# A window attention and two dense layers on one core: the first layer's low product moves to GpSimd, more words are joined there, and sums of weights are kept in DRAM

## The chip, the cores and the metric

One core of one Trainium2 chip runs the whole program. Its engines are TensorE (matrix products, PE in the profile, with PEld for the loading of weights), VectorE (DVE), ScalarE (ACT), GpSimd (POOL) and the queue that issues transfers (SP). The metric is the device time of one execution in microseconds, the median of the runs.

## What is computed

The inputs are q, k and v (float32; 4 batches, 8 heads, 576 positions, 64 columns) and two layers' weights (float64). Cut to what matters:

```python
scores = scale * q @ k.T                       # per batch and head
scores = where(0 <= i - j < 128, scores - slope[head] * (i - j), -1e9)
x = softmax(scores) @ v                        # as 2304 tokens x 512

h = x @ w_in                                   # first layer, 512 -> 2048
P = a0 + a1*h + a2*h**2 + a3*h**3
Q = 1 + |b0|*|h| + |b1|*h**2
y = (P / (Q + 1e-6)) @ w_out                   # 2048 -> 512

h = y @ w2_in                                  # second layer, 512 -> 2048
out = where(h > 0, h, exp(min(h, 0)) - 1) @ w2_out
```

## The kernel before

The weights arrive as pairs of 32-bit words of a float64. A float32 is joined from the two: ScalarE scales the high word (`conv_scale`, `join_scale`), VectorE shifts the low word, sets its bits in and sets the sign (three operations, `conv_shift`, `conv_or`, `conv_sign`, or all of `join_words`). Each float32 operand of a product is then split into a high part that TensorE can take and a low part, the difference from it; a product is three matmuls, high x high, low x high and high x low (`PASS`).

**Attention** (0 to about 155 us) works through 16 units of two heads by an order written out by hand (`STEPS`), with the words of the first layer's weights joined beside it. The words of the last four pairs of keys come by `conv_step`, six of whose calls stand at the end of attention and the rest in the first block of the first layer; the low part (`conv_lo`) was GpSimd's there.

**The first layer** (about 155 to 560 us) takes the 2304 tokens in 6 blocks of 384 columns (`j`) and the 2048 hidden columns in 16 chunks of 128 (`f`), 96 steps `s` in all. In step s TensorE runs `gemm1` for chunk s (12 matmuls into one of four banks, h) and `gemm2_T` for chunk s - 3 (12 matmuls that need the chunk's high and low product). `rational(s)` is the work between them: ScalarE forms the square, the Abs, two linear terms, and the logarithm and exponential that give 1/Q; VectorE forms the denominator of chunk s, and for chunk s - 1 the high product `hi` (L286), a correction (L298, L304) and the low product `lo` (L308), and between them, for chunk s, the numerator (L302, which reads h from PSUM, and L306). At the end of a block `split_x` splits the next block's x (four high parts on ScalarE, four low parts on VectorE, L224), since there is room for one block's. In blocks 1 to 5, the steps with f not divisible by 3 and below 15 join half a word of the second layer's weights, 40 halves in all; these go to DRAM as float32 (`joined`). In the last block `prepare` forms the second layer's first sums and splits.

**The second layer** (from about 555 us) takes the tokens in three rounds J of two blocks, and the hidden columns in 8 pairs p of two chunks, 24 pairs q in all. A pair's seven products come from sums and differences of weights (`sum_w`, four per pair, on GpSimd) and of x (`sum_x`, four pairs of rows per round, on GpSimd but in the first), each split into high and low (`hi_w`, `hi_op`, `lo`). Results are added up on VectorE (L943), go through the exponential on ScalarE and VectorE (L958), are split, and are multiplied by the second weights in the next pair (`gemm2`). Twelve of the 16 second words (`raw_ones`) were joined in the first round (`join_wo`) and kept in DRAM. The steps stand in a table (`step`) with engine, cost and needs; `in_order` lays out one order for all engines from these costs. Each engine's queue is worked off in that order.

Of the kernel before, what the change touches and what calls it, by code (L numbers as in the profile page):

```python
# [11 lines left out]
I32 = mybir.dt.int32  # L12
# [32 lines left out]
def kernel(  # L45
# [90 lines left out]
    def conv_shift(key):  # L136
        low, _ = words(key)
        nc.vector.tensor_scalar(
            out=low, in0=low, scalar1=29, scalar2=None, op0=ALU.logical_shift_right
        )  # L140

# [28 lines left out]

    stage = {"scaled": None, "whole": None}

    def conv_step(keys, more=True):
# [89 lines left out]
    def rational(c, old=True, beside=None):  # L263
# [17 lines left out]
        if old:  # L281
            qq0, ee0, rr0 = q_t.pop(c - 1)
            hi = row(f"ghi{(c - 1) % 4}", F32R)
            lo = row(f"glo{(c - 1) % 4}", F32R)
            g_t[c - 1] = (hi, lo)
            nc.vector.tensor_tensor(out=hi, in0=ee0, in1=rr0, op=ALU.mult)  # L286
        if new:
            nc.vector.scalar_tensor_tensor(  # L288
                out=qq, in0=h2, scalar=b_abs[:, 1:2], in1=qq, op0=ALU.mult, op1=ALU.add
            )  # L290
            rr = row(f"rr{c % 2}")
# [3 lines left out]
        if beside:  # L295
            beside()
# [382 lines left out]
    def experts():  # L679
# [46 lines left out]
        joined, half, two, whole, pair = {}, {}, {}, [], []  # L726
        OPS, XO, sums, G, sq, low_part = {}, {}, {}, {}, {}, {}
# [3 lines left out]
        early_ones = [("wi", KF + f) for f in range(KF)] + [("wo", KF + 2 * p) for p in range(4)]  # L731

        def load_half(n):
# [4 lines left out]
            half[n] = t = cv_tile([P, PC], I32, "half", 2 * (n % 2))  # L738
# [12 lines left out]
        def join_scale(n):  # L751
# [3 lines left out]
            if not whole:  # L755
                whole.append(cv_tile([P, 2, HC], F32, "whole", 1))
            w = whole[0][:, n % 2]
            nc.scalar.activation(out=w, in_=high.bitcast(F32), func=AF.Copy, scale=2.0 ** -112)

        def join_words(n):  # L760
            t = half.pop(n).rearrange("p (c t) -> p c t", t=2)
            low, high = t[:, :, 0], t[:, :, 1]
            w = whole[0][:, n % 2]
            nc.vector.tensor_scalar(
                out=low, in0=low, scalar1=29, scalar2=None, op0=ALU.logical_shift_right
            )
            wi = w.bitcast(I32)
            nc.vector.scalar_tensor_tensor(
                out=wi, in0=wi, scalar=3, in1=low, op0=ALU.logical_shift_left, op1=ALU.bitwise_or
            )  # L770
            nc.vector.scalar_tensor_tensor(
# [50 lines left out]
        def sum_w(q, eng=nc.gpsimd):  # L822
            w = two[q]
            a11, a12, a21, a22 = [w[:, e, h * HC:(h + 1) * HC] for e in range(2) for h in range(2)]
            sq[q] = s = [cv_tile([P, 2, HC], F32, "s", n) for n in range(2)]
            for n, (x, y, op) in enumerate((
                (a21, a22, ALU.add), (s[0][:, 0], a11, ALU.subtract), (a11, a21, ALU.subtract),
                (a12, s[0][:, 1], ALU.subtract),
            )):
                eng.tensor_tensor(out=s[n // 2][:, n % 2], in0=x, in1=y, op=op)  # L830

# [21 lines left out]
        def sum_x(J, n, eng=nc.gpsimd):  # L853

            if J == 0:
# [5 lines left out]
            for k in range(2):  # L861
# [142 lines left out]
        def weight_steps(w):  # L1004
# [5 lines left out]
            if w > 0:  # L1010
# [3 lines left out]
                step((w, "sum"), "POOL", 2900, lambda: sum_w(w), (w, "load"), (w - 1, "lo", "C"), (w - 1, "lo", "D"))  # L1014
# [26 lines left out]
        def x_sums(J):  # L1041

            used = [("xlo", J - 1, nm, k) for nm in ORDER for k in range(2)]
            for n in range(4):
                step(("sum", J, n), "POOL", 2300, lambda n=n: sum_x(J, n), *used, *[("sum", J, i) for i in range(n)])

        def second(q):
# [25 lines left out]
            if q == 0:  # L1073
                x_steps(0, ("t1", "t4", "b22"), -1)
# [5 lines left out]
            if p == NP2 - 1 and q + 1 < NQ:  # L1080
                x_sums(q // NP2 + 1)
                x_steps(q // NP2 + 1, ORDER, q)

        def in_order():
# [20 lines left out]
            free = {"PE": 0, "ACT": 1500, "DVE": 2500, "POOL": 0, "SP": 0}  # L1105
# [35 lines left out]
        def prepare(f):  # L1141

            if f == 1:
                load_wi(0)
            if 3 <= f < 7:
                sum_x(0, f - 3, nc.vector)
            if f == 7:
                sum_w(0, nc.vector)
            if 8 <= f < 12:
                hi_w(0, "ABCD"[f - 8])  # L1150
                lo((0, "ABCD"[f - 8]))
            if 7 <= f < 11:
                for k in range(2):
                    hi_op(0, ORDER[f - 7], k)
                for k in range(2):
                    lo((0, ORDER[f - 7], k))
# [72 lines left out]
```

## Time and profile before

| | us |
|---|---|
| median of 3 runs | 968.08 (966.07 to 968.5) |
| the profiled execution | 965.85 |
| its span, first to last instruction | 963.8 |
| TensorE busy | 927.3 (96%) |
| VectorE busy | 864.8 (90%) |
| ScalarE busy | 750.6 (78%) |
| GpSimd busy | 232.7 (24%) |

Busy times are of the profiled execution. TensorE's share is a mean over stages, and matmuls overlap, so the waits of a stage tell more than its busy share.

### The profile page before, as it was taken

The numbers are of one execution on the slowest core, as the hardware profiler recorded it, in microseconds if no ns is written. First come the engines' busy times: TensorE is split into PE (matmuls) and PEld (weight loads), VectorE is DVE, ScalarE is ACT, GpSimd is POOL, SyncE is SP. The second block draws the span as 40 slices with busy tenths as digits, with TensorE's granted clock in tenths as the row PEclk, the third lists the DMA queues.
The fourth block names the chain that finished last, engine by engine and source line by source line (L and its number), as shares of the span: only waits on it lengthen the run. The fifth ranks groups of instructions, "written<-read, shape, count | busy, mean of one in ns | idle before, by whom it ended". The sixth has DMA issues, their size and how long they took to land.

```text
span 963.8 us, 16615 instructions
## 1 busy us (share of the span) xinstructions
PE 927.3 (96%) x5494; PEld 842.7 (87%) x5494; DVE 864.8 (90%) x1949; ACT 750.6 (78%) x1628; POOL 232.7 (24%) x296
## 2 busy tenths in 40 slices
PE   7999999999999999999999979899989999999998
PEld 4776668999999999999999978788978989989897
DVE  5999989999999999999999999999988768887753
ACT  5999999889889888888887967666866657766553
POOL 4777764110000000000000152332254221133100
PEclk9999999999999999999999979999999999999999
DMA  6899842001221212211100124243332221322101
GB/s 169 213 236 247 218 131 82 1 23 33 67 66 50 67 50 66 66 50 60 62 28 1 56 69 129 98 140 113 99 121 86 57 77 56 103 94 78 55 1 66
DMA packets 102486, 83.92 MB, mean 87 GB/s; under 512 B 61696, under 2 KB 83200, under 8 KB 102400
## 3 DMA queue, kind: packets, MB, share of 16 engines
q1 hardware_dynamic: 102400, 82.87, 29.7%
q8 instruction: 43, 0.70, 0.3%
q14 instruction: 43, 0.35, 0.1%
HBM read 69.73 MB, written 13.11 MB: 86 GB/s over the span
## 4 chain that ended last, share of the span: by engine, by line
PE 56%; DVE 20%; ACT 13%; issue 7%; SPq 2%; DMA 1%; DVEq 0%; ACTq 0%
PE acc L691 15%; PE h L248 14%; PE acc L903 14%; PE m L887 12%; ACT pT L427 2%; ACT pr_wo L501 2%; ACT pr_wi L501 2%; DVE qq L288 2%; DVE ghi L286 2%; DVE qq L298 2%; DVE op_wo L847 1%; DVE op_wi L847 1%; DVE oo L302 1%; SPq L334 1%; DVE ee L943 1%
## 5 line engine op out<-in xcount | busy, mean ns | idle before, releaser
L248 PE MATMUL h<-xs,w_wi 128*128 128x384 f32 x1152 | 218.1, 335 | 3.9 <-DVE xs L224 3.4
L248 PEld LDWEIGHTS h<-xs,w_wi 128*128 128x128 f32 x1152 | 200.5, 188 | 6.8 <-DVE xs L224 5.3
L691 PE MATMUL acc<-ghi,w_wo 128*128 128x384 f32 x768 | 196.2, 336 | 0.0
L830 POOL TENSOR_TENSOR s<-two_wo 128x256 f32<-128x256 f32 x32 | 33.3, 1041 | 503.5 <-DMA two_wo<-joined_wi 379.6
L691 PEld LDWEIGHTS acc<-ghi,w_wo 128*128 128x128 f32 x768 | 139.8, 189 | 0.0
L691 PE MATMUL acc<-glo,w_wo 128*128 128x384 f32 x384 | 129.6, 338 | 1.8 <-DVE glo L308 1.8
L887 PE MATMUL m<-xo_wo,op_wi 128*128 128x384 f32 x336 | 79.1, 343 | 12.1 <-DVE ee L943 4.8
L903 PE MATMUL acc<-op_wo,ghi 128*128 128x512 f32 x288 | 89.6, 392 | 0.0
L292 ACT ACTIVATE rr<-qq,c_q 128x384 f32<-128x384 f32 x96 | 59.0, 614 | 27.6 <-DVE qq L288 23.7
L887 PEld LDWEIGHTS m<-xo_wo,op_wi 128*128 128x128 f32 x336 | 60.9, 191 | 20.2 <-DVE ee L943 6.4
L887 PE MATMUL m<-xo_wi,op_wi 128*128 128x384 f32 x336 | 78.2, 341 | 0.0
L691 PEld LDWEIGHTS acc<-glo,w_wo 128*128 128x128 f32 x384 | 72.7, 189 | 3.4 <-DVE glo L308 3.3
L274 ACT ACTIVATE qq<-h,b_abs 128x384 f32<-128x384 f32 x96 | 55.4, 577 | 23.8 <-DVE ee L304 23.8
L275 ACT ACTIVATE oo<-h,a_sb 128x384 f32<-128x384 f32 x96 | 68.0, 708 | 0.7 <-DVE ee L306 0.5
L278 ACT ACTIVATE ee<-h,a_sb 128x384 f32<-128x384 f32 x96 | 67.1, 699 | 0.5 <-DVE glo L308 0.5
L288 DVE SCALAR_TENSOR_TENSOR qq<-h,b_abs,qq 128x384 f32<-128x384 f32 x96 | 60.9, 635 | 5.6 <-ACT qq L274 5.6
L949 ACT ACTIVATE oo<-qq 128x384 f32<-128x384 f32 x24 | 12.6, 525 | 64.7 <-DVE qq L943 64.7
L887 PEld LDWEIGHTS m<-xo_wi,op_wi 128*128 128x128 f32 x336 | 61.4, 190 | 0.0
L903 PEld LDWEIGHTS acc<-op_wo,ghi 128*128 128x128 f32 x288 | 53.5, 188 | 8.9
L903 PE MATMUL acc<-op_wo,glo 128*128 128x512 f32 x144 | 57.0, 396 | 0.0
L943 DVE TENSOR_TENSOR ee<-ee,m 128x384 f32<-128x384 f32 x96 | 52.4, 545 | 4.2 <-PE m L887 4.2
L306 DVE TENSOR_TENSOR ee<-ee,oo 128x384 f32<-128x384 f32 x96 | 54.5, 568 | 0.2
(196 smaller groups left out, 2279.5 us busy)
## 6 DMA issues: line engine op xcount, KB each, us to landing
raw_wo<-in_moe_w_out_dram SPq DMA_DIRECT2D x25, 512.0 KB, 4.8
pair<-joined_wo SPq DMA_DIRECT2D x36, 256.0 KB, 2.7
raw_wi<-in_moe_w_in_dram SPq DMA_DIRECT2D x16, 512.0 KB, 4.3
half<-in_moe_w_in_dram SPq DMA_DIRECT2D x32, 256.0 KB, 2.8
two_wo<-joined_wi SPq DMA_DIRECT2D x32, 256.0 KB, 2.9
v<-in_v_dram SPq DMA_DIRECT2D x32, 128.0 KB, 3.0
joined_wi<-whole SPq DMA_DIRECT2D x32, 128.0 KB, 1.8
two_wi<-joined_wi SPq DMA_DIRECT2D x16, 256.0 KB, 3.0
```

What stands on the lines that cost most here:

```text
L248: nc.tensor.matmul(h, lhsT=WT["wi", f][:, SEL[wp], kk * P:(kk + 1) * P], rhs=x[xp][kk], start=(kk == 0 and n == 0), stop=(kk == KD - 1 and ...
L274: nc.scalar.activation(out=qq, in_=h, func=AF.Abs, scale=b_abs[:, 0:1])
L275: nc.scalar.activation(out=oo, in_=h2, func=AF.Identity, scale=a_sb[:, 3:4], bias=a_sb[:, 1:2])
L278: nc.scalar.activation(out=ee, in_=h2, func=AF.Identity, scale=a_sb[:, 2:3], bias=a_sb[:, 0:1])
L288: nc.vector.scalar_tensor_tensor(out=qq, in0=h2, scalar=b_abs[:, 1:2], in1=qq, op0=ALU.mult, op1=ALU.add)
L292: nc.scalar.activation(out=rr, in_=qq, func=AF.Ln, bias=c_q)
L306: nc.vector.tensor_tensor(out=ee, in0=ee, in1=oo, op=ALU.add)
L501: nc.scalar.activation(out=probs(u, n), in_=probs(u, n), func=AF.Exp, scale=-1.0, bias=mx[:, n:n + 1], accum_out=sm[:, n:n + 1],)
L691: nc.tensor.matmul(acc_t[d], lhsT=WT["wo", f][:, SEL[wp], d * P:(d + 1) * P], rhs=gt[SEL[xp]], start=(f == 0 and n == 0), stop=(f == KF - ...
L887: nc.tensor.matmul(out, lhsT=w[:, SEL[wp], c0:c0 + P], rhs=XO[q // NP2, nm, k][:, SEL[xp]], start=(k == 0 and n == 0), stop=(k == 1 and n ...
L903: nc.tensor.matmul(acc_t[T, t], lhsT=gt[SEL[xp]][:, t * P:(t + 1) * P], rhs=w[:, SEL[wp]], start=(first and n == 0), stop=(last and n == 2),)
L943: nc.vector.tensor_tensor(out=t, in0=R[q, x], in1=M[q, m], op=ALU.add)
```

## The change

- The first layer's low product is formed by GpSimd from chunk 4 on, and stands ahead of the two operations that form the numerator; those now work in place in h's bank in PSUM. The Abs result goes to a bank of PSUM (6) from chunk 4 on. h has three banks (4, 5, 7) and the products three pairs of tiles.
- The work that stands beside `rational` comes in up to three pieces at fixed places (`beside`), and ScalarE's copies behind the exponential (`after`). `conv_step` can leave its pieces to these places; its low part is VectorE's.
- Halves of words are joined in 13 of 16 steps of blocks 1 to 4 and in two of block 5: 54 halves, the 16 words of w2_in and 11 of w2_out, with three tiles for the loaded halves. Five words of w2_out are left to the second layer.
- In the last block the first sums, splits and weight sums come one piece at a time from a list (`AT_DVE`, `AT_ACT`).
- The sums of weights of the first round are stored in DRAM (`keep_sums`) and loaded in the second and third (`load_sums`). The second pair's sums are VectorE's. GpSimd's sums of x wait for the first product of later pairs.
- The products of the first pair go to other banks (`m_first`), and the planner starts from other times for ScalarE and VectorE.

```diff
-    def conv_step(keys, more=True):
+    def conv_step(keys, more=True, later=False):
+        while put_off:
+            go_on()
...
         if scaled:
-            conv_shift(scaled)
-            conv_or(scaled)
-            conv_sign(scaled)
+            put_off.append(lambda: conv_shift(scaled))
+            put_off.append(lambda: conv_or(scaled))
+            put_off.append(lambda: conv_sign(scaled))
         if whole:
-            conv_lo(whole)
+            put_off.append(lambda: conv_lo(whole, "D"))
+        while put_off and not later:
+            go_on()
...
-    def rational(c, old=True, beside=None):
+    def rational(c, old=True, beside=3 * (lambda: None,), after=lambda: None):
...
+            ee = row(f"ee{c % 2}")
             qq = row(f"qq{c % 2}")
+            qa = bank(6, [P, TB], "qa") if c > 3 else qq
             oo = row("oo")
-            ee = row(f"ee{c % 2}")
+            rr = row(f"rr{c % 2}")
             nc.scalar.activation(out=h2, in_=h, func=AF.Square)
-            nc.scalar.activation(out=qq, in_=h, func=AF.Abs, scale=b_abs[:, 0:1])
+            nc.scalar.activation(out=qa, in_=h, func=AF.Abs, scale=b_abs[:, 0:1])
...
-            hi = row(f"ghi{(c - 1) % 4}", F32R)
-            lo = row(f"glo{(c - 1) % 4}", F32R)
-            g_t[c - 1] = (hi, lo)
+            hi = row(f"ghi{(c - 1) % 3}", F32R)
+            low = row(f"glo{(c - 1) % 3}", F32R)
+            g_t[c - 1] = (hi, low)
             nc.vector.tensor_tensor(out=hi, in0=ee0, in1=rr0, op=ALU.mult)
+        beside[0]()
         if new:
             nc.vector.scalar_tensor_tensor(
-                out=qq, in0=h2, scalar=b_abs[:, 1:2], in1=qq, op0=ALU.mult, op1=ALU.add
+                out=qq, in0=h2, scalar=b_abs[:, 1:2], in1=qa, op0=ALU.mult, op1=ALU.add
             )
...
-        if beside:
-            beside()
+        after()
+        beside[1]()
         if old:
             nc.vector.scalar_tensor_tensor(
                 out=qq0, in0=qq0, scalar=EPSC, in1=hi.bitcast(F32), op0=ALU.add, op1=ALU.mult
             )
-        if new:
-            nc.vector.tensor_tensor(out=oo, in0=oo, in1=h, op=ALU.mult)
+        beside[2]()
         if old:
             nc.vector.tensor_tensor(out=ee0, in0=ee0, in1=qq0, op=ALU.subtract)
+            (nc.gpsimd if c > 4 else nc.vector).tensor_tensor(out=low, in0=ee0, in1=rr0, op=ALU.mult)
         if new:
-            nc.vector.tensor_tensor(out=ee, in0=ee, in1=oo, op=ALU.add)
-        if old:
-            nc.vector.tensor_tensor(out=lo, in0=ee0, in1=rr0, op=ALU.mult)
+            nc.vector.tensor_tensor(out=h, in0=oo, in1=h, op=ALU.mult)
+            nc.vector.tensor_tensor(out=ee, in0=ee, in1=h, op=ALU.add)
...
-        early_ones = [("wi", KF + f) for f in range(KF)] + [("wo", KF + 2 * p) for p in range(4)]
+        early_ones = [("wi", KF + f) for f in range(KF)] + [("wo", KF + f) for f in range(11)]
...
-            half[n] = t = cv_tile([P, PC], I32, "half", 2 * (n % 2))
+            half[n] = t = cv_tile([P, PC], I32, "half", n % 3)
...
+        def keep_sums(w):
+            kept[w] = [dram.tile([P, PC], F32, name=f"sums_{w}_{n}") for n in range(2)]
+            for d, t in zip(kept[w], sq[w]):
+                nc.sync.dma_start(out=d, in_=t.rearrange("p s c -> p (s c)"))
+
+        def load_sums(w):
+            sq[w] = [cv_tile([P, 2, HC], F32, "s", n) for n in range(2)]
+            for d, t in zip(kept[w % NP2], sq[w]):
+                nc.sync.dma_start(out=t.rearrange("p s c -> p (s c)"), in_=d)
...
-        ny = cycle((0, 1))
+        m_banks = cycle((6, 7))
+        m_first = [7, 4, 6, 7, 4, 6, 7]
...
-            out = bank((4 if q == 0 else 6) + next(ny), [P, TB], "m")
+            out = bank(m_first.pop(0) if m_first else next(m_banks), [P, TB], "m")
...
-            if w > 0:
+            if w == 0:
+                step((w, "kept"), "SP", 1200, lambda: keep_sums(w))
+            else:
...
-                step((w, "sum"), "POOL", 2900, lambda: sum_w(w), (w, "load"), (w - 1, "lo", "C"), (w - 1, "lo", "D"))
+                gone = [(w - 1, "lo", "C"), (w - 1, "lo", "D")]
+                if w >= NP2:
+                    step((w, "sum"), "SP", 1200, lambda: load_sums(w), *gone)
+                else:
+                    eng, cost, at = (nc.vector, 1400, "DVE") if w == 1 else (nc.gpsimd, 3500, "POOL")
+                    step((w, "sum"), at, cost, lambda: sum_w(w, eng), (w, "load"), *gone, (w - 1, "kept"))
+                    step((w, "kept"), "SP", 1200, lambda: keep_sums(w), (w, "sum"))
...
-        def x_sums(J):
+        def x_sums(J, q):
...
-                step(("sum", J, n), "POOL", 2300, lambda n=n: sum_x(J, n), *used, *[("sum", J, i) for i in range(n)])
+                step(("sum", J, n), "POOL", 2300, lambda n=n: sum_x(J, n), *used, (q - 4 + n, "b11"),
+                     *[("sum", J, i) for i in range(n)])
...
-            free = {"PE": 0, "ACT": 1500, "DVE": 2500, "POOL": 0, "SP": 0}
+            free = {"PE": 0, "ACT": 3400, "DVE": 5500, "POOL": 0, "SP": 0}
...
+        AT_ACT = {6: x_hi(0, 0, 1), 9: w_hi("AB"), 10: x_hi(1, 0, 1), 11: w_hi("C") + x_hi(2, 0),
+                  12: x_hi(2, 1) + w_hi("D"), 13: x_hi(3, 0, 1), 14: x_hi(4, 0, 1)}
+        AT_DVE = [lambda n=n, k=k: sum_x(0, n, nc.vector, (k,)) for n in range(4) for k in range(2)]
+        AT_DVE += [lambda: lo((0, ORDER[0], 0)), lambda: lo((0, ORDER[0], 1))]
+        AT_DVE += [lambda n=n: sum_w(0, nc.vector, (n,)) for n in range(4)]
+        AT_DVE += [lambda key=key: lo(key) for key in (
+            (0, "A"), (0, "B"), (0, ORDER[1], 0), (0, ORDER[1], 1), (0, "C"), (0, ORDER[2], 0),
+            (0, ORDER[2], 1), (0, "D"), (0, ORDER[3], 0), (0, ORDER[3], 1), (0, ORDER[4], 0), (0, ORDER[4], 1),
+        )]
...
+        def joins(s):
+
+            return s >= KF and s % KF not in (0, 8, KF - 1) and s < LAST + 3
...
             if s >= 4:
-                run_all(gemm1(s, f, x1[j], 4 + s % 4))
+                run_all(gemm1(s, f, x1[j], (4, 5, 7)[(s - 4) % 3]))
...
-            if j > 0 and f % 3 and f < KF - 1 and nj < 2 * len(early_ones):
-                rational(s, beside=lambda: join_words(nj))
+            if joins(s):
+                rational(s, beside=(lambda: join_shift(nj), lambda: join_words(nj), lambda: join_sign(nj)))
                 nj += 1
+            elif s >= LAST:
+                prepare(s)
             else:
-                rational(s)
+                rational(s, beside=(go_on, go_on, go_on))
```

## Rows read from the trace of the kernel before

**Rows 1.** Busy time by stretch: stretch, its length, each engine's busy us, clock, DMA share, GB/s.
```profile
226.00:540.00 314.00, 311.07 (x1788) 309.38 (x1786) 305.70 (x674) 270.77 (x528) 0.00 (x0) 1.00 0.17 51
580.00:725.00 145.00, 136.26 (x665) 119.55 (x665) 136.07 (x239) 100.63 (x201) 46.13 (x43) 1.00 0.34 112
725.00:964.00 239.00, 235.30 (x1162) 210.22 (x1160) 174.93 (x314) 147.15 (x291) 49.45 (x52) 1.00 0.22 68
```

**Rows 2.** TensorE's waits, 160 to 580, then 580 to 725: total us, times, longest.
```profile
PE m L887 <- ACT qq L937: 3.7, 1, 3.7
PE h L248 <- DVE xs L224: 3.4, 5, 0.8
PE acc L691 <- DVE glo L308: 1.8, 4, 0.8
PE m L887 <- DVE qq L943: 1.6, 1, 1.6
...
PE m L887 <- DVE ee L943: 6.8, 5, 2.4
PE m L887 <- DVE qq L943: 1.7, 3, 0.9
```

**Rows 3.** Busy time of the stretch after TensorE's longest wait, columns as in rows 1.
```profile
563.80:573.40 9.60, 7.95 (x24) 7.44 (x25) 9.43 (x18) 6.57 (x15) 2.82 (x3) 0.50 0.00 1
```

**Rows 4.** Timeline of one joining step, VectorE then gemm1: start us, us, engine, line, operation.
```profile
263.07 0.55 DVE L286 TENSOR_TENSOR ghi<-ee,rr 128x384 fp32r<-128x384 f32 x1
263.54 0.61 DVE L288 SCALAR_TENSOR_TENSOR qq<-h,b_abs,qq 128x384 f32<-128x384 f32 x1
264.06 0.29 DVE L764 TENSOR_SCALAR half<-half 128x256 int32<-128x256 int32 x1
...
265.19 0.55 DVE L298 SCALAR_TENSOR_TENSOR qq<-qq,ghi 128x384 f32<-128x384 f32 x1
265.66 0.55 DVE L302 TENSOR_TENSOR oo<-oo,h 128x384 f32<-128x384 f32 x1
...
267.06 0.55 DVE L308 TENSOR_TENSOR glo<-ee,rr 128x384 fp32r<-128x384 f32 x1
267.53 0.55 DVE L286 TENSOR_TENSOR ghi<-ee,rr 128x384 fp32r<-128x384 f32 x1
...
262.90 2.24 PE L248 MATMUL h<-xs,w_wi 128*128 128x384 f32 x12
...
267.06 2.24 PE L248 MATMUL h<-xs,w_wi 128*128 128x384 f32 x12
```

**Rows 5.** Timeline where GpSimd and VectorE overlap; one row gives a line's ns min/median/max.
```profile
550.67 2.62 POOL L830 TENSOR_TENSOR s<-two_wo 128x256 f32<-128x256 f32 x1 [340.01 <-DMA two_wo<-joined_wi]
...
556.30 7.70 POOL L866 TENSOR_TENSOR xT<-xT 128x384 f32<-128x384 f32 x6
...
557.97 1.36 DVE L286 TENSOR_TENSOR ghi<-ee,rr 128x384 fp32r<-128x384 f32 x1
...
561.80 0.54 DVE L302 TENSOR_TENSOR oo<-oo,h 128x384 f32<-128x384 f32 x1
...
577.30 0.69 DVE L847 TENSOR_TENSOR op_wo<-s,op_wo 128x512 fp32r<-128x512 f32 x1
...
578.07 0.73 POOL L830 TENSOR_TENSOR s<-two_wo 128x256 f32<-128x256 f32 x1 [5.30 <-DVE op_wo L847]
...
L866 POOL TENSOR_TENSOR xT<-xT x16: 1011/1321/1462, 556.3 to 710.2; 128x384 f32<-128x384 f32 x16
```

**Rows 6.** Timeline, one word's joining and the next operation; the page's DMA row.
```profile
587.76 0.41 DVE L138 TENSOR_SCALAR raw_wo<-raw_wo 128x512 int32<-128x512 int32 x1
...
589.55 0.55 DVE L943 TENSOR_TENSOR ee<-ee,m 128x384 f32<-128x384 f32 x1
...
two_wo<-joined_wi SPq DMA_DIRECT2D x32, 256.0 KB, 2.9
```

**Rows 7.** Timeline, a VectorE operation beside a word's low part on GpSimd.
```profile
209.42 1.65 DVE L288 SCALAR_TENSOR_TENSOR qq<-h,b_abs,qq 128x384 f32<-128x384 f32 x1
```

More of the change, by code (lines that the diff above doesn't have):

```diff
@@ L134, in conv_scale, with shift @@
             nc.scalar.activation(out=t, in_=high, func=AF.Copy, scale=2.0 ** -112)
-    def conv_shift(key):
-        low, _ = words(key)
+    def shift(low):
         nc.vector.tensor_scalar(
@@ L140, in conv_shift @@
         )
+    def conv_shift(key):
+        shift(words(key)[0])
     def conv_or(key):
@@ L725, in experts @@
         dram = ctx.enter_context(tc.tile_pool(name="dram", bufs=1, space=bass.MemoryType.DRAM))
-        joined, half, two, whole, pair = {}, {}, {}, [], []
-        OPS, XO, sums, G, sq, low_part = {}, {}, {}, {}, {}, {}
-        early_ones = [("wi", KF + f) for f in range(KF)] + [("wo", KF + 2 * p) for p in range(4)]
+        joined, half, two, whole, pair = {}, {}, {}, {}, []
+        OPS, XO, sums, G, sq, kept, low_part = {}, {}, {}, {}, {}, {}, {}
+        early_ones = [("wi", KF + f) for f in range(KF)] + [("wo", KF + f) for f in range(11)]
         def load_half(n):
@@ L754, in join_scale, with join_shift @@
             high = half[n].rearrange("p (c t) -> p c t", t=2)[:, :, 1]
-            if not whole:
-                whole.append(cv_tile([P, 2, HC], F32, "whole", 1))
-            w = whole[0][:, n % 2]
+            whole[n] = w = row("glo3" if n % 2 else "ghi3")[:, 0:HC]
             nc.scalar.activation(out=w, in_=high.bitcast(F32), func=AF.Copy, scale=2.0 ** -112)
+        def join_shift(n):
+            shift(half[n].rearrange("p (c t) -> p c t", t=2)[:, :, 0])
         def join_words(n):
[L761 to L767, printed above, removed]
+            low = half[n].rearrange("p (c t) -> p c t", t=2)[:, :, 0]
+            wi = whole[n].bitcast(I32)
             nc.vector.scalar_tensor_tensor(
@@ L770, in join_words, with join_sign @@
             )
+        def join_sign(n):
+            high = half.pop(n).rearrange("p (c t) -> p c t", t=2)[:, :, 1]
+            w = whole.pop(n)
+            wi = w.bitcast(I32)
             nc.vector.scalar_tensor_tensor(
@@ L851, in x_row, with sum_x @@
             return xT[:, k, c0:c0 + TB]
-        def sum_x(J, n, eng=nc.gpsimd):
-            if J == 0:
+        def sum_x(J, n, eng=nc.gpsimd, ks=range(2)):
+            if 0 not in ks:
+                pass
+            elif J == 0:
                 nm = "_".join(map(str, t_slots[n]))
@@ L860, in sum_x @@
                 sums[J, n] = [x_row(J - 1, k + 2 * (n // 2), n % 2) for k in range(2)]
-            for k in range(2):
+            for k in ks:
                 b11, b21, b12, b22 = [x_row(J, k + 2 * i, T) for T in range(2) for i in range(2)]
@@ L1073, in second @@
             if q == 0:
-                x_steps(0, ("t1", "t4", "b22"), -1)
+                x_steps(0, ("t4", "b22"), -1)
             if q > 0 and p == 0:
@@ L1139, in last_pair, with x_hi, w_hi, prepare @@
                     put_out(NQ, T, t, "AD"[t % 2])
-        def prepare(f):
-            if f == 1:
-                load_wi(0)
[L1145 to L1156, printed above, removed]
+        def x_hi(n, *ks):
+            return [lambda k=k: hi_op(0, ORDER[n], k) for k in ks]
+        def w_hi(names):
+            return [lambda x=x: hi_w(0, x) for x in names]
+        AT_ACT = {6: x_hi(0, 0, 1), 9: w_hi("AB"), 10: x_hi(1, 0, 1), 11: w_hi("C") + x_hi(2, 0),
[7 more added lines that the diff above has]
+        )]
+        def prepare(s):
+            f = s - LAST
+            if f == 3:
+                load_wi(0)
             if f == 14:
@@ L1160, in prepare, with copies, next_one @@
                     load_raw(0, e)
+            def copies():
+                for fn in AT_ACT.get(f, []):
+                    fn()
+            def next_one():
+                if f >= 3 and AT_DVE:
+                    AT_DVE.pop(0)()
+            rational(s, beside=(lambda: None, next_one, next_one), after=copies)
+        def joins(s):
+            return s >= KF and s % KF not in (0, 8, KF - 1) and s < LAST + 3
         SK = 3
```

33 lines of the change are left out of this document (19 added, 14 removed).

## The prediction

> **What bounds the kernel now.** I read the busy times by stretch first. From 226 to 540 us, blocks 1 to 4 of the first layer's six and most of block 5, TensorE is busy 311.1 of 314 us and VectorE 305.7, so both are near their end. From 580 to 725 us TensorE loses 8.7 us while VectorE is busy 136.1 of 145. From 725 us on VectorE is busy 174.9 of 239 [rows 1]. Then I read TensorE's waits in the same stretches: all are put down to VectorE, but for one on ScalarE. Up to 580 us they are five of 3.4 us for the low parts of the next block's x and four of 1.8 us for a low product (5.2 us in the first layer), and at the handover to the second layer 3.7 + 1.6 = 5.3. From 580 to 725 they are eight, 6.8 + 1.7 = 8.5 us. After 725 us there is none [rows 2]. [...] What can be won is thus 5.2 + (5.3 + 4.0) + 8.5 = 23 us, and a stage with no wait gives nothing.
>
> **The first layer's count.** Two starts of gemm1 stand 4.16 us apart, which is TensorE's step. VectorE's step with a join runs from 263.07 to 267.53, 4.46 us. Its join (three operations, 264.06 to 265.19) is 1.13 of that, so the seven arithmetic operations are 3.33, most of them 0.47 apart [rows 4]. A block of 16 steps with 10 joins and four low parts of x (4 x 0.47) is 16 x 3.33 + 10 x 1.13 + 1.9 = 66.5 us for VectorE against 16 x 4.16 = 66.6 for TensorE: level, which is why it comes late to each block's end.
>
> **The low product goes to GpSimd.** One operation fewer leaves 2.86 a step; 13 joins in place of 10 come in. A block is 16 x 2.86 + 13 x 1.13 + 1.9 = 62.4 us: 4.2 us spare, 0.26 a step. GpSimd isn't free to VectorE, though. Six of its 384-wide products in a row took 7.70 us, 1.28 each, against 1.01 at the least; a VectorE product beside them that reads two operands in SBUF took 1.36 for 0.55, while one that reads h from PSUM took 0.54 [rows 5]. So each GpSimd product holds up such an operation by up to 0.81 us, and PSUM operands escape. The new order uses that: behind the subtraction that feeds the low product stand two operations with h in PSUM, then the next high product. The subtraction is done 0.55 after its start, GpSimd starts 0.08 later (its row at 578.07 begins 0.08 after the operation at 577.30 ended) [rows 5] and ends at 0.55 + 0.08 + 1.01 = 1.64; the next high product is due at 3 x 0.47 = 1.41. The delay is between 0 and 0.23 a step; I take 0.13, because the hold of 0.81 is shorter than the 1.01. That is 2.1 us a block, and 2.1 stay spare: TensorE remains the bound.
>
> Three operations change sides: the Abs result is written to PSUM and read there, the product with h is written to PSUM, the last sum reads it there. No row writes PSUM from ScalarE or VectorE. The nearest are the step's own 384-wide operations, 0.47 to 0.52 apart whether they read h or not [rows 4], so I allow -0.05 to +0.05 each, -0.15 to +0.15 a step, and take 0.
> [...]
>
> The buffers shrink: h has three banks in place of four, the products three pairs of tiles. VectorE's step for the chunk that gemm1 finished before 262.90 ends about 267.1, also with its last read of h put at the end; the gemm1 that asks for the bank again starts at 267.06 + 4.16 = 271.2 [rows 4]: 4.1 us of cover. The high product at 263.07 writes a tile that gemm2 has left by 262.90 - 4.16 = 258.7: 4.3 us. Both cost nothing unless VectorE falls a whole step behind. ScalarE's Abs no longer waits for the old subtraction.
>
> With 1.2 us spare in each of the three steps without joins around a block's end, VectorE reaches the low parts of x early, and the low products, now behind fewer operations, too. Of 5.2 us I take **4.7**, bounds 0 and 5.2.
>
> **Joins.** 52 steps in blocks 1 to 4 and two in block 5 take exactly 54 halves: 27 of the 32 words. That moves seven words out of the second layer, at 1.79 us of VectorE each (587.76 to 589.55) [rows 6], 12.5 us. Loads of halves stand one step further ahead on SP, in a third tile, so nothing new waits there.
>
> **Block 5** hands VectorE 26 pieces in 13 steps: 18 of 384 columns (18 x 0.47 = 8.5) and, scaled by columns, five of 256 and three of 512 (5 x 0.31 + 3 x 0.63 = 3.4), 12 us; 13 x (2.86 + 0.13) + 12 = 50.9 us against 54.1. ScalarE carries up to two copies a step, as it does now.
>
> **The handover.** Before, GpSimd forms the second pair's weight sums from 550.67 (its first product needed 2.62 us to get in) and six x differences from 556.30, beside VectorE's last steps [rows 5]; their holds slow these. The long wait is for the copy that frees the first product's bank. Now the weight sums of that pair are VectorE's (4 x 0.31 = 1.2 us), the differences wait for the first product of pairs 3 to 6, and the third product has a bank of its own. Left near the end are the low products. Of 9.3 us I take **7.8** and leave 1.5 for the chain copy, sum, product; bounds 0 and 9.3.
>
> **580 to 725 us.** VectorE loses most of 12.5 us of words here. It keeps holds of up to 0.81 us from GpSimd's weight sums; of the two runs of eight x differences, the first comes to stand here (8 x 0.81 = 6.5 us at most), while the second, which ends about 711 us now [rows 5], leaves for pairs 11 to 14, where VectorE has a quarter of its time free [rows 1]. So 12.5 us fewer in 145, and VectorE goes from 94% to about 85%. TensorE's waits won't all go, since the order of the steps is laid out by estimated costs: of 8.5 us I take **5.8**, bounds 0 and 8.5.
>
> **Sums kept in DRAM.** 16 of 24 sums become two loads each on SP. Each waits there for the low parts of the pair before, and loads of weights and the output's stores stand behind it; ScalarE's copies of these sums wait for its landing, 2.9 us by the page's like loads [rows 6], in place of GpSimd's work. TensorE waits for nothing after 725 us, so I take 0; one load that is late on the path costs up to 2.9. The store of the first sums holds up VectorE's new sums, and all queued behind them, for at most the same; the sums are due a pair later: 0.
>
> **The words of the first layer** (eight low parts, GpSimd to VectorE): 8 x 0.69 = 5.5 us more of VectorE, by the 512-wide row at 577.30 [rows 5], less the stretch that they cause now, as 1.65 for 0.61 at 209.42 [rows 7], 8 x 1.04 = 8.3. Half lies at the end of attention; I take 0, bounds -1 and +1.
>
> **Sum.** 4.7 + 7.8 + 5.8 = 18.3 us. The profiled execution took 965.85 (span 963.8), so 947.55. The median of the runs, 968.08, is 2.23 above it: **949.8**. With all of it gained it is 968.1 - 23 - 1 = 944.
>
> **Rivals.** (a) The handover stays as long, since the second layer's first chain is short of another thing (the pair's load, which needs the last block's x gone, or ScalarE's copies): 949.8 + 7.8 = 957.6. For it: sums, splits and loads for the first two pairs all come due within one pair's time there. Against it: the longest wait is for the bank whose sharing now ends, the other for VectorE. (b) The margin is eaten without more: the three operations at +0.05 and the delay at 0.23 make 0.38 against 0.26 spare, 0.12 x 16 = 1.9 us in each of four blocks, and the block ends stay: 949.8 + 7.7 + 4.7 = 962.2. (c) **Slower:** the low product comes late and meets the next high product in full. At 0.81 a step, four blocks lose 16 x (0.81 - 0.26) = 8.8 each; block 5 is 16 x (2.86 + 0.81) + 2 x 1.13 + 12 = 73.0, 6.4 over; block 0, with four words at 1.79 + 0.61 and 1.9 for x, is 70.2, 3.6 over: 45 us against the 7.8 + 5.8 = 13.6 gained elsewhere, 999. It decides from 0.46 a step (4 x (16 x 0.46 - 4.2) + 0.8 = 13.4). For it: GpSimd's first product at 550.67 was held off while VectorE worked on SBUF operands back to back; a low product that starts so meets one operation after the other. Against it: it starts beside PSUM operands.
> [...]
>
> **How the numbers follow.** Forecast 0.60; (a) 0.14; (b) 0.14; (c) 0.12. About 0.3%, 2.9 us, is what a measurement of this kernel can tell from no change. Forecast, (a) and a little over half of (b) are faster, 0.82; the rest of (b) within, 0.06; (c) slower, 0.12. From 944 to 966 the range holds the forecast's bounds, (a) and most of (b), about 0.8.
>
> **What would show it.** Right: no wait for xs at block ends; the high product 0.55 to 0.8 long, the two operations with h 0.54; GpSimd's low products about 1.0; no granted clock of 0.50 after 540 us; waits between 580 and 725 us under 3 us. Wrong: high products above 1.0 and gemm2 waiting for glo, a gap at the handover, or waits for the kept sums after 725 us.

## The result and the profile after

The changed kernel takes 952.22 us in the median (950.8 to 953.21, 4 runs), the kernel before 967.08 beside it (4 runs): ratio 0.9845 [0.9823, 0.9866], 14.9 us less, where 18.3 were forecast. The profiled execution took 951.87 (span 950.2 against 963.8).

Busy time by stretch of the changed kernel (stretch, its length, each engine's busy us with instructions in the order PE, PEld, DVE, ACT, POOL, then clock, DMA share, GB/s), to be read beside [rows 1]:
```profile
145.00:165.00 20.00, 17.33 (x147) 15.04 (x146) 17.92 (x34) 17.66 (x36) 4.84 (x5) 1.00 0.33 102
226.00:540.00 314.00, 313.91 (x1807) 312.65 (x1806) 292.27 (x647) 276.70 (x548) 76.19 (x75) 1.00 0.22 68
540.00:580.00 40.00, 37.67 (x207) 35.88 (x206) 38.81 (x76) 32.43 (x68) 10.39 (x10) 1.00 0.35 120
580.00:725.00 145.00, 137.96 (x678) 121.72 (x677) 130.43 (x222) 98.49 (x200) 43.20 (x36) 1.00 0.43 134
725.00:930.00 205.00, 205.00 (x1019) 184.45 (x1018) 145.94 (x280) 127.46 (x257) 0.00 (x0) 1.00 0.30 93
```
TensorE's waits in the changed kernel (what waited, for whom, us in total, times, longest), from 160 to 580 us, then from 580 to 950, beside [rows 2]:
```profile
PE m L918 <- DVE ee L974: 2.3, 1, 2.3
PE acc L705 <- DVE glo L319: 0.5, 1, 0.5
PE h L260 <- ACT xs L235: 0.5, 1, 0.5
PE h L260 <- DVE xs L236: 0.4, 1, 0.4
PE acc L705 <- POOL glo L319: 0.2, 1, 0.2
...
PE m L918 <- DVE ee L974: 3.8, 4, 1.8
PE m L918 <- DVE qq L974: 3.0, 2, 2.9
```
Three sums follow. In the first layer 5.2 us of waits became 0.5 + 0.5 + 0.4 + 0.2 = 1.6: 3.6 gained. From 226 to 540 us TensorE now lacks 0.09 us of 314. At the handover 5.3 us of waits and, by estimate, 4.0 lost at a clock of 0.50 (half of the 7.95 us busy there [rows 3]) became one wait of 2.3 with the clock at 1.00 behind it: 7.0 gained. From 580 to 725 us 8.5 became 3.8 + 3.0 = 6.8: only **1.7** gained, though VectorE was freed of seven words.

These make 12.3 of the span's 13.6 us. The rest fits the end of attention, where the clock was lower before. The kernel before, busy time by stretch:
```profile
150.00:155.00 5.00, 3.02 (x19) 2.40 (x19) 4.72 (x8) 4.57 (x10) 2.24 (x2) 0.90 0.33 105
155.00:162.00 7.00, 7.00 (x58) 6.71 (x58) 6.76 (x10) 5.93 (x12) 3.01 (x2) 0.83 0.22 78
```
Microsecond by microsecond the clock there was 0.50 to 0.51 from 154 to 157 us and 0.78 in the next. By estimate from the means, 0.83 over 7 us is 0.17 x 7 = 1.2 us lost, and 0.90 over 5 us is 0.5. The changed kernel has 1.00 there. Its longest wait in that place is 2.1 us against 2.0. Eight of the runs below leave attention as the change has it, and in four of them the clock over 155 to 162 us was 0.76 to 0.82 all the same; the run with all sums on VectorE:
```profile
155.00:162.00 7.00, 7.00 (x56) 6.42 (x57) 5.70 (x12) 5.92 (x12) 0.00 (x0) 0.76 0.38 118
```
So these 1.7 us are the clock behind a like wait and nothing that the diff does: in the profiled execution they are luck.

### The profile page after: what moved, and what is told of

It is laid out like the page before. It is cut to its first block, busy times and chain, and to the rows that moved or that the text cites. A ratio compares the mean times of both kernels' runs of the same rounds, so it can differ in the third digit from the quotient of the medians.

```text
span 950.2 us, 16856 instructions
## 1 busy us (share of the span) xinstructions
PE 920.9 (97%) x5494; PEld 839.0 (88%) x5494; DVE 818.8 (86%) x1890; ACT 745.1 (78%) x1635; POOL 248.6 (26%) x312
## 4 chain that ended last, share of the span: by engine, by line
PE 63%; DVE 18%; ACT 14%; issue 4%; DMA 1%; POOL 0%; SPq 0%; DVEq 0%; ACTq 0%; POOLq 0%
PE acc L934 17%; PE h L260 15%; PE acc L705 15%; PE m L918 14%; ACT pT L441 2%; ACT pr_wo L515 2%; ACT pr_wi L515 2%; DVE ghi L301 2%; DVE qq L304 1%; DVE ee L322 1%; DVE ee L318 1%; DVE qq L313 1%; DVE h L321 1%; DVE op_wi L875 1%; DVE op_wo L875 1%
## 5 line engine op out<-in xcount | busy, mean ns | idle before, releaser
L319 POOL TENSOR_TENSOR glo<-ee,rr 128x384 fp32r<-128x384 f32 x92 | 93.5, 1016 | 315.8 <-DVE ee L318 160.9
L918 PE MATMUL m<-xo_wo,op_wi 128*128 128x384 f32 x336 | 77.1, 337 | 7.2 <-DVE ee L974 4.0
L301 DVE TENSOR_TENSOR ghi<-ee,rr 128x384 fp32r<-128x384 f32 x96 | 53.6, 558 | 12.2 <-ACT oo L290 0.5
L322 DVE TENSOR_TENSOR ee<-ee,h 128x384 f32<-128x384 f32 x96 | 53.2, 555 | 10.0
L304 DVE SCALAR_TENSOR_TENSOR qq<-h,b_abs,qa 128x384 f32<-128x384 f32 x92 | 55.9, 608 | 3.7 <-ACT qa L289 3.7
```

The source lines that it names most:

```text
L304: nc.vector.scalar_tensor_tensor(out=qq, in0=h2, scalar=b_abs[:, 1:2], in1=qa, op0=ALU.mult, op1=ALU.add)
L319: (nc.gpsimd if c > 4 else nc.vector).tensor_tensor(out=low, in0=ee0, in1=rr0, op=ALU.mult)
L322: nc.vector.tensor_tensor(out=ee, in0=ee, in1=h, op=ALU.add)
L918: nc.tensor.matmul(out, lhsT=w[:, SEL[wp], c0:c0 + P], rhs=XO[q // NP2, nm, k][:, SEL[xp]], start=(k == 0 and n == 0), stop=(k == 1 and n ...
```

## The experiments

All times are medians, and each ratio is to the kernel before on the same chip. Each expectation names its theories for itself.

| kernel | us | ratio [95%] |
|---|---|---|
| as changed | 952.22 | 0.9845 [0.9823, 0.9866] |
| third round's x differences on VectorE | 950.65 | 0.9826 [0.9807, 0.9845] |
| all x differences and weight sums on VectorE | 944.79 | 0.9762 [0.9743, 0.9781] |
| all x differences alone on VectorE | 945.25 | 0.9777 [0.9764, 0.979] |
| sums of weights not kept | 953.66 | 0.9856 [0.9836, 0.9875] |
| second round's differences at once | 954.18 | 0.9863 [0.9844, 0.9881] |
| third product in a shared bank | 956.41 | 0.9878 [0.9857, 0.99] |
| 40 halves in place of 54 | 961.39 | 0.9945 [0.9929, 0.9961] |
| low product on VectorE | 1016.29 | 1.0505 [1.0471, 1.0538] |
| numerator in SBUF | 995.94 | 1.0297 [1.0273, 1.0321] |
| all sums on VectorE, nine products in other banks | 942.21 | 0.974 [0.9727, 0.9753] |

### Where the gain from 580 to 725 us went

GpSimd's timeline of the changed kernel has its x differences (L896) here (start, us, operation, count, what it waited for):
```profile
603.23 2.62 POOL L896 TENSOR_TENSOR xT<-xT 128x384 f32<-128x384 f32 x2
...
635.66 4.92 POOL L896 TENSOR_TENSOR xT<-xT 128x384 f32<-128x384 f32 x4
672.56 7.60 POOL L896 TENSOR_TENSOR xT<-xT 128x384 f32<-128x384 f32 x6 [31.98 <-DVE xo_wo L875]
688.93 4.04 POOL L896 TENSOR_TENSOR xT<-xT 128x384 f32<-128x384 f32 x2 [8.78 <-DVE xo_wo L875]
```
The prediction had the second run of eight "leave for pairs 11 to 14", past 725 us. It runs at 672 and 689, in the full stretch, and waits for tiles that VectorE frees, not for a product of a later pair. The new need, `(q - 4 + n, "b11")`, orders the plan. There is no data behind it, so on the chip a difference is held back only by VectorE's last reads of the rows that it overwrites (L875 above) and by what stands ahead of it in GpSimd's own queue. For the second round that is weight sums; for the third, whose sums are loaded, nothing.

What such a run does to VectorE shows at the longest wait. Changed kernel, timeline of VectorE, then of TensorE:
```profile
637.32 1.23 DVE L875 TENSOR_TENSOR op_wo<-two_wo,op_wo 128x256 fp32r<-128x256 f32 x1
638.48 1.25 DVE L137 TENSOR_SCALAR raw_wi<-raw_wi 128x512 int32<-128x512 int32 x1
639.83 1.29 DVE L147 SCALAR_TENSOR_TENSOR pair<-pair,raw_wi 128x512 int32<-128x512 int32 x1
...
642.36 0.79 PE L918 MATMUL m<-xo_wo,op_wi 128*128 128x384 f32 x3 [2.86 <-DVE qq L974]
```
While GpSimd forms four differences (635.66 to 640.58) a VectorE operation of 256 columns takes 1.23 us (0.41 at 593.77 in the same trace), and right behind them TensorE stands for 2.86.

**Third round's differences on VectorE.**
```diff
-                step(("sum", J, n), "POOL", 2300, lambda n=n: sum_x(J, n), *used, (q - 4 + n, "b11"),
+                eng, at, cost = (nc.vector, "DVE", 940) if J == 2 else (nc.gpsimd, "POOL", 2300)
+                step(("sum", J, n), at, cost, lambda n=n, eng=eng: sum_x(J, n, eng), *used, (q - 4 + n, "b11"),
```


> The eight differences of x for the third round go from GpSimd to VectorE, with the same place in the plan. Theory A: the need of a later pair's first product orders only the plan, and GpSimd, which has nothing else to do by then, ran them at 672 to 693 us beside VectorE, whose operations they held up; on VectorE they really stand at pairs 11 to 14, where a quarter of its time is free. Then TensorE's wait of 1.75 us near 683 goes and the time is about 2 us less than the changed kernel's 952.2: 950. Rival B: that wait is VectorE's own load of low parts there; the time stays at 952.

Measured 950.65. The differences as a group by tile, and TensorE's waits behind 580 us, in this kernel:
```profile
L896 DVE TENSOR_TENSOR xT<-xT x8: 551/552/555, 734.8 to 782.4; 128x384 f32<-128x384 f32 x8
...
PE m L918 <- DVE qq L974: 3.0, 2, 2.9
PE m L918 <- DVE ee L974: 1.7, 1, 1.7
```
On VectorE the same steps do stand where the plan has them, 735 to 782 us. The waits are 4.7 in place of 6.8: 2.1 us of the missing gain was the third round's place. The medians differ by 1.6 us and their intervals overlap, so it is the waits that show it.

**All differences and weight sums on VectorE** (`sum_x` for every round and `sum_w` with `nc.vector`).
```diff
+                step(("sum", J, n), "DVE", 940, lambda n=n: sum_x(J, n, nc.vector), *used, (q - 4 + n, "b11"),
...
+                    eng, cost, at = nc.vector, 1400, "DVE"
```


> All of the second layer's sums and differences that GpSimd still forms (six pairs' weight sums, two rounds' x differences) go to VectorE; GpSimd does nothing there. Theory A: a GpSimd operation costs VectorE more in holds (0.5 to 0.8 us) than the operation itself would (0.34 or 0.47), so VectorE's busy time falls and TensorE's waits between 580 and 725 us go from 6.8 to under 3 us: about 948. Rival B: VectorE, busy 130 of 145 us there, takes on 6 x 4 x 0.34 + 8 x 0.47 = 12 us more and the waits grow: 955 or more.

Measured 944.79. Busy time by stretch, and TensorE's one wait of the second layer with the clock around it:
```profile
580.00:725.00 145.00, 145.00 (x722) 130.55 (x721) 130.29 (x263) 102.08 (x205) 0.00 (x0) 1.00 0.45 147
...
568.48 0.76 PE L918 MATMUL m<-xo_wo,op_wi 128*128 128x384 f32 x3 [2.25 <-DVE ee L974]
...
566.00:578.00 12.00, 9.74 (x42) 8.68 (x41) 10.51 (x22) 8.85 (x19) 0.00 (x0) 0.86 0.26 78
```
TensorE loses nothing from 580 to 725 us any more. VectorE forms the weight sums and the second round's differences there itself (the third round's stand past 725 us again), 263 operations against 222, and is busy 130.29 us against 130.43. The same 145 us also hold more of the program, 722 matmuls against 678. So GpSimd's operations cost VectorE at least as much in holds as they took off it, and made it late in places.

**All x differences alone on VectorE**, the weight sums of pairs 2 to 7 left on GpSimd.
```diff
+                step(("sum", J, n), "DVE", 940, lambda n=n: sum_x(J, n, nc.vector), *used, (q - 4 + n, "b11"),
```


> Both later rounds' differences of x go to VectorE; the weight sums of pairs 2 to 7 stay on GpSimd. It splits the gain of all sums on VectorE (944.8 against 952.2) between the two kinds. If each GpSimd operation costs VectorE its hold: 16 of 384 columns are gone (about 0.8 us each), 24 of 256 columns stay (about 0.5 to 0.6 each), so about half of the gain comes: 947 to 949, and the wait of 1.7 us near 594 us, beside a pair's weight sums, stays. Rival: only the differences matter, 945, or only the weight sums, 952.

Measured 945.25, better than expected, and not to be told from 944.79. So the differences carry nearly all; of the waits past 580 us one of 1.7 at 594 is left, beside GpSimd's weight sums (588.74 to 593.25 in this run).

**Sums of weights not kept**: GpSimd forms them in all pairs, as before.
```diff
-                if w >= NP2:
-                    step((w, "sum"), "SP", 1200, lambda: load_sums(w), *gone)
...
+                step((w, "sum"), at, cost, lambda: sum_w(w, eng), (w, "load"), *gone)
```


> The sums of weights are neither stored nor loaded: GpSimd forms them in all 24 pairs (VectorE for the second pair). Prediction's step: the kept sums are worth nothing, 952 within 1 us, because TensorE waits for nothing after 725 us. Theory A adds: GpSimd's queue now has sums of pairs 8 and later ahead of the third round's differences, so these run after 725 us and the wait near 683 us goes: 950 to 951. Rival: the kept sums carry part of the gain: 954 or more, with new waits after 700 us.

Measured 953.66, 1.4 us above the change, which their overlapping intervals can't tell from nothing, and between the expectations. GpSimd's timeline has the first of the third round's differences here, two in a row:
```profile
735.95 2.62 POOL L896 TENSOR_TENSOR xT<-xT 128x384 f32<-128x384 f32 x2
```
The last two start at 783.60. With weight sums ahead of them in GpSimd's queue, the differences come where the prediction put them. So keeping the sums is what drew the third round's differences forward. Its waits past 580 us are 5.5, not 6.8; in its profile the clock was 0.96 over 540 to 580 us, where the changed kernel had 1.00, which may be why the time did not fall with them.

**Second round's differences at once**: the need on a later product for the third round only.
```diff
-                step(("sum", J, n), "POOL", 2300, lambda n=n: sum_x(J, n), *used, (q - 4 + n, "b11"),
+                at = [(q - 4 + n, "b11")] if J == 2 else []
+                step(("sum", J, n), "POOL", 2300, lambda n=n: sum_x(J, n), *used, *at,
```


> The second round's differences of x lose their need of the first products of pairs 3 to 6, so the plan lets GpSimd start them as soon as the first round's splits are done, near 563 us. If GpSimd's operations beside VectorE at the handover are what made the gap and the half clock there: a gap comes back behind 563 us, several us of waits, less what now goes at 603 to 642 us (2.9 us): 954 to 958. Rival: the new banks and the even preparation closed the gap, and where the differences stand is indifferent: 952.

Measured 954.18. GpSimd's six differences are back at the handover, and TensorE waits behind them (timelines of GpSimd and TensorE, and the stretch behind):
```profile
560.01 7.88 POOL L896 TENSOR_TENSOR xT<-xT 128x384 f32<-128x384 f32 x6
572.25 1.30 PE L918 MATMUL m<-xo_wo,op_wi 128*128 128x384 f32 x3 [6.64 <-DVE ee L974]
572.00:582.00 10.00, 9.75 (x38) 9.14 (x39) 8.18 (x13) 5.58 (x13) 6.42 (x6) 0.73 0.33 102
```
That is a loss as at the handover of the kernel before, a wait and a lower clock (0.73 above, 0.50 there [rows 3]), though the wait is for VectorE and not for ScalarE's copy. But the waits at 603 to 642 us are gone (3.7 past 580 in place of 6.8): the change mostly moved this loss.

**Third product in a shared bank.**
```diff
-        m_first = [7, 4, 6, 7, 4, 6, 7]
+        m_first = [7, 4, 7, 4, 7, 4, 7]
```


> The first pair's products take two banks in turn (7 and 4), so that the third product waits again for ScalarE's copy out of the first one's bank. If that bank is what made the 3.7 us wait before: a wait on ScalarE's copy returns at the handover, 1 to 4 us: 953 to 956. Rival: the copy was late only because VectorE was late, and is in time now: 952.

Measured 956.41. Timeline of TensorE, then two stretches:
```profile
559.62 1.33 PE L918 MATMUL m<-xo_wo,op_wi 128*128 128x384 f32 x3 [1.79 <-DVE qq L974]
559.00:569.00 10.00, 9.38 (x46) 9.39 (x47) 8.64 (x19) 6.23 (x14) 1.00 (x1) 0.83 0.25 71
648.00:656.00 8.00, 8.00 (x33) 6.83 (x32) 5.54 (x11) 2.72 (x5) 0.00 (x0) 0.78 0.49 157
```
The wait for ScalarE's copy, to which the prediction put down the long wait, is 0.3 us here. The wait at 559.62 replaces the one at 567.66, and the waits' sum is that of the change (2.1 and 6.8 us against 2.3 and 6.8). What is added is a lower clock behind two waits, 0.83 and 0.78 above where the changed kernel has 1.00 in both stretches: the two executions with a mean clock of 0.994 and 0.996 took 953.35 and 952.83, the other three (0.989 to 0.992) 956.41 to 957.62. What the bank is worth by itself stays open; shared banks together with the early differences, as before the change, were not run.

**40 halves**: the words of the change before, 20 in place of 27.
```diff
-        early_ones = [("wi", KF + f) for f in range(KF)] + [("wo", KF + f) for f in range(11)]
+        early_ones = [("wi", KF + f) for f in range(KF)] + [("wo", KF + 2 * p) for p in range(4)]
...
-            return s >= KF and s % KF not in (0, 8, KF - 1) and s < LAST + 3
+            return s >= KF and s % KF not in (0, 8, KF - 1) and s < LAST + 3 and nj < 2 * len(early_ones)
```


> Only the 40 halves of before are joined in the first layer, so that seven words (1.79 us of VectorE each) return to the second layer; VectorE has 14 x 0.88 us less to do in the first layer, where TensorE does not wait. If these words are what made TensorE wait there: waits between 560 and 725 us grow by 3 to 8 us: 955 to 960. Rival: the words fitted into VectorE's free time: 952.

Measured 961.39, past the dear end. TensorE's waits past 580 us:
```profile
PE m L918 <- DVE qq L974: 6.7, 3, 2.7
PE m L918 <- DVE ee L974: 6.0, 6, 1.8
```
12.7 us against 6.8, so the seven words are worth 5.9 us of waits there, close to the 5.8 that the forecast took for the whole stretch. The time is 9.2 us longer: the handover's wait is 0.6 longer (2.9), and the clock, 0.96 over 540 to 580 and 0.99 over 580 to 725 us, makes about 3 us by estimate. The kernel before had these words and 8.5: by the waits, the rest of the change made this stretch worse by about 4 us and the words paid for it.

### What the low product needs

**Low product on VectorE**, in the new order.
```diff
-            (nc.gpsimd if c > 4 else nc.vector).tensor_tensor(out=low, in0=ee0, in1=rr0, op=ALU.mult)
+            nc.vector.tensor_tensor(out=low, in0=ee0, in1=rr0, op=ALU.mult)
```


> The first layer's low product stays on VectorE, in the new order of steps, all else as changed. If moving it is what keeps VectorE under TensorE's step: the steps of chunks 4 and 5, where it was still VectorE's, are 4.07 us apart without a join, with one about 4.7; a block is 13 x 4.7 + 3 x 4.07 + 1.9 = 75 us against 66.6, some 8 to 9 us more in each block: 990 to 1005. Rival: the order and the thinned joins carry the first layer and the move is worth little: under 960.

Measured 1016.29, beyond what was expected. VectorE's timeline, and the largest of TensorE's waits:
```profile
264.07 0.56 DVE L318 TENSOR_TENSOR ee<-ee,qq 128x384 f32<-128x384 f32 x1
264.73 0.56 DVE L319 TENSOR_TENSOR glo<-ee,rr 128x384 fp32r<-128x384 f32 x1
265.20 0.56 DVE L321 TENSOR_TENSOR h<-oo,h 128x384 f32<-128x384 f32 x1
...
PE acc L705 <- DVE glo L319: 16.8, 42, 1.1
```
Here the operation that reads what the one right before it wrote starts 0.66 behind it (264.07 to 264.73), the independent one 0.47 (to 265.20). A join step is 4.83 us (262.40 to 267.23), against 4.46 in the old order [rows 4]: the new order by itself is worse, and pays only with the low product elsewhere. The clock adds to the time: its mean is 0.978 over the span of 1016.3 us, against 0.996 over 950.2 in the changed kernel, by estimate 22 us lost against 4.

**Numerator in SBUF**: the product with h and the sum in tiles of SBUF.
```diff
-            nc.vector.tensor_tensor(out=h, in0=oo, in1=h, op=ALU.mult)
-            nc.vector.tensor_tensor(out=ee, in0=ee, in1=h, op=ALU.add)
+            nc.vector.tensor_tensor(out=oo, in0=oo, in1=h, op=ALU.mult)
+            nc.vector.tensor_tensor(out=ee, in0=ee, in1=oo, op=ALU.add)
```


> The two operations behind the low product write and read the numerator in SBUF again (as before the change) in place of h's bank; the low product stays on GpSimd. If GpSimd holds up only operations with two operands in SBUF: the last sum (two SBUF operands) now falls into GpSimd's hold and takes about 1.0 us in place of 0.55, a join step goes from 4.15 to about 4.5 us, and blocks 1 to 5 lose some 5 us each: 970 to 980. Rival: where the operands lie does not matter: 952.

Measured 995.94, far past the expectation. Timelines of GpSimd and VectorE:
```profile
262.91 1.01 POOL L319 TENSOR_TENSOR glo<-ee,rr 128x384 fp32r<-128x384 f32 x1 [3.62 <-DVE ee L318]
263.31 1.03 DVE L322 TENSOR_TENSOR ee<-ee,oo 128x384 f32<-128x384 f32 x1
264.47 0.56 DVE L301 TENSOR_TENSOR ghi<-ee,rr 128x384 fp32r<-128x384 f32 x1
```
With two operands in SBUF beside the low product the sum takes 1.03 in place of 0.55, and the next high product stands 1.16 behind it. This is the hold of rival (c), met by the sum in place of the next high product: 0.47 a step comes on top of 0.41 that the new order costs (below), less the 0.26 that a join got cheaper in 13 of 16 steps. That is 0.67 past the forecast's count, beyond the 0.46 from which that rival decides, and the kernel is slower than before.

With h in PSUM the same sum is 0.55 (266.71 in the changed kernel, beside GpSimd's product of 266.30 to 267.32). Two operands in SBUF are not needed for a hold, though: the shift shown above, which reads one tile in SBUF, was held too (1.25 at 638.48 beside GpSimd's differences, against 0.42 at 645.30 with GpSimd idle).

### The best of both

**All sums on VectorE, and nine first products in other banks.**
```diff
-        m_first = [7, 4, 6, 7, 4, 6, 7]
+        m_first = [7, 4, 6, 7, 4, 6, 7, 5, 4]
...
```
The rest of its edit is that of all sums on VectorE.

> All sums on VectorE, and in addition the second pair's first two products go to banks 5 and 4, which are free by then, in place of 6 and 7. The wait that is left at the handover, 2.25 us at 568, is for VectorE's read of the bank that the sixth product filled one product earlier. If that bank is all that it waits for: the wait goes, and with it the granted clock of 0.50 behind it, 2 to 3 us: 942. Rival: the product needs VectorE's other work of that time as well, and the wait only moves by a product: 944 to 945.

Measured **942.21**, the fastest: 10 us below the change. The profiled execution was the slowest of five, 945.52; its first gemm1 starts at 145.6 us against 142.6 with all sums on VectorE, so that the 3 us lie in attention. The handover by stretch:
```profile
540.00:580.00 40.00, 39.88 (x221) 38.21 (x220) 38.54 (x80) 34.83 (x72) 6.10 (x6) 1.00 0.29 93
```
Against the run with all sums on VectorE only the banks differ: its wait at 568 us and the lower clock behind it (0.86 over 566 to 578 us) are gone, and past 580 us 0.4 us is left. The two medians are 2.6 us apart with intervals that overlap a little.

## Why the prediction was right, and where it was not

The direction was right, and the time, 952.2, lies 2.4 above the forecast. Of the three parts of the sum, the first layer and the handover came out near their sizes, the one by errors that cancel, the other for one of the two reasons given; the third did not. The nearness of the whole is in part luck: the 1.7 us of clock at the end of attention stand in no term.

**First layer: 3.6 for 4.7, on a thinner margin and by errors that cancel.** A join step and GpSimd's product in the changed kernel (VectorE's timeline, then GpSimd's), against [rows 4]:
```profile
263.24 0.56 DVE L301 TENSOR_TENSOR ghi<-ee,rr 128x384 fp32r<-128x384 f32 x1
263.72 0.29 DVE L137 TENSOR_SCALAR half<-half 128x256 int32<-128x256 int32 x1
263.92 0.61 DVE L304 SCALAR_TENSOR_TENSOR qq<-h,b_abs,qa 128x384 f32<-128x384 f32 x1
264.44 0.42 DVE L778 SCALAR_TENSOR_TENSOR ghi<-ghi,half 128x256 int32<-128x256 int32 x1
264.78 0.55 DVE L313 SCALAR_TENSOR_TENSOR qq<-qq,ghi 128x384 f32<-128x384 f32 x1
265.25 0.42 DVE L786 SCALAR_TENSOR_TENSOR ghi<-half,ghi 128x256 int32<-128x256 int32 x1
265.58 0.55 DVE L318 TENSOR_TENSOR ee<-ee,qq 128x384 f32<-128x384 f32 x1
266.05 0.55 DVE L321 TENSOR_TENSOR h<-oo,h 128x384 f32<-128x384 f32 x1
266.71 0.55 DVE L322 TENSOR_TENSOR ee<-ee,h 128x384 f32<-128x384 f32 x1
267.40 0.56 DVE L301 TENSOR_TENSOR ghi<-ee,rr 128x384 fp32r<-128x384 f32 x1
...
266.30 1.02 POOL L319 TENSOR_TENSOR glo<-ee,rr 128x384 fp32r<-128x384 f32 x1 [3.14 <-DVE ee L318]
```
The step is 4.16 us, of which three terms were mis-sized. The delay by GpSimd, 0.13 in the sum, is 0: the two operations with h and the high product behind them are all 0.55 to 0.56 long. The new order's price was missed: product, sum and next high product hang on one another, so they stand 0.66 and 0.69 apart and not 0.47, 0.41 a step more. This is not GpSimd's doing: with the low product on VectorE they stand 0.66 and 0.69 apart as well (265.20, 265.86 and 266.55 there). Nor is it PSUM's: with the numerator in SBUF product and sum stand 0.65 apart (262.66, 263.31). In the changed kernel it is there in a step without GpSimd's product:
```profile
165.58 0.55 DVE L321 TENSOR_TENSOR h<-oo,h 128x384 f32<-128x384 f32 x1
166.24 0.56 DVE L322 TENSOR_TENSOR ee<-ee,h 128x384 f32<-128x384 f32 x1
166.89 0.56 DVE L301 TENSOR_TENSOR ghi<-ee,rr 128x384 fp32r<-128x384 f32 x1
```
The join, in three pieces between independent operations, costs 0.20 + 0.34 + 0.33 = 0.87 and not 1.13. The cheaper join and the delay that did not come gave back most of what the order added, which the prediction didn't foresee. With 3.41 for a step without a join (289.10 to 292.51) a block is 13 x 4.16 + 3 x 3.41 + 1.9 = 66.2 us of VectorE against TensorE's 66.6: 0.4 us spare, not 2.1. VectorE's busy share of 93% from 226 to 540 us hides this, since most of its idle time, 17.3 of 21.7 us, is the gap ahead of the sum (L322) and the high product (L301), which read what the operation before them wrote, and in this order nothing fills it. The PSUM operands, taken at 0, cost at most 0.01 us of an operation's own time: from 226 to 540 us product and sum take 0.554 and 0.555 in the mean, against 0.546 and 0.550 before, the denominator 0.607 against 0.611, and ScalarE's Abs 0.545 against 0.578.

**Handover: 7.0 for 7.8, right in size, not in its reason.** The 4.0 in the prediction's 5.3 + 4.0 is an estimate: the clock was 0.50 behind the long wait, where TensorE was busy 7.95 us [rows 3], and in the changed kernel it is 1.00 over 566 to 574 us, behind its wait there. The long wait was put down to the bank that a copy frees. Undoing the third bank brought back 0.3 us of that wait; letting GpSimd form six differences there again brought back 6.64 us. That GpSimd slows VectorE's last steps, the prediction's other reason, is the one that the runs show.

**580 to 725 us: 1.7 for 5.8, the step that failed.** The words were worth what the forecast took for the stretch (5.9 by the run with 40 halves). What failed is the step that "the second run of eight x differences leaves for pairs 11 to 14", and with it "VectorE goes from 94% to about 85%": it was 90%. Both runs of eight stayed in this stretch, and the first at 603 to 640 us brought its own waits. The forecast left 2.7 us of waits, and 6.8 came. 2.1 of them go when the third round's differences leave the stretch (6.8 to 4.7). The other 4.7 stand beside the second round's differences (3.0 go with these) and the weight sums (1.7): the prediction had counted their holds as VectorE's time, but made the waits behind them too small. All of it off GpSimd, the stretch loses nothing: with 8.5 us to win, the prediction's upper bound was there to be had.

**Kept sums and words of the first layer at 0.** TensorE loses nothing from 725 to 930 us, and the run without kept sums is level. That the kept sums empty GpSimd's queue, and so let the differences forward, the prediction missed. The low parts that went to VectorE were not tried alone; the waits at the end of attention are as before within 0.6 us.

**Rivals.** (a) did not come. (b) did not either, but was near: 0.4 us of a block's margin is left. (c)'s hold came only in the run with the numerator in SBUF, which takes away what the new order rests on.

## What to carry to other kernels

GpSimd helped VectorE here where its product stands beside operations with a PSUM operand and off the path (a sum of 0.55 us beside it, 1.03 with both operands in SBUF); beside a full VectorE with operands in SBUF, doing the work on VectorE itself was faster by 7 us (944.79 against 952.22). Where a plan gives an operation a need with no data behind it, ask what holds it back on its own engine's queue: if nothing does, it will run early, as the third round's differences did at 672 and 689 us. When counting a busy VectorE, count for a 384-column operation right behind the one that it reads from what it took here, 0.59 (290.10 to 290.69 in the changed kernel) to 0.69 us, and not 0.47, and put independent pieces between the two.

## What the runs showed of the hardware that was not expected

The same wait was followed by the lower clock in one execution and not in another. A wait of 2.26 us at 567.66 left the clock at 1.00 in the changed kernel; one of 2.25 at 568.48 with all sums on VectorE left 0.86 over 566 to 578, where three matmuls together took up to 1.16 us against 0.68. The wait of 2.86 at 642 us was followed by 1.00 in the changed kernel and by 0.83 over 640 to 650 with the third round's differences on VectorE. At the end of attention a wait of 2.0 to 2.1 was followed by 0.83 before the change and 1.00 after. What a wait of 2 to 3 us costs thus isn't its length alone, and in one profile each, one or two us between kernels can be the clock.
